# Attention through packed queries, then a squared-ReLU MLP: the order of the first loads, the zero matmuls and the planner's priorities are changed

## The chip, the cores and the metric

The kernel runs on one core of one Trainium2 chip. The metric is the device time of one execution in microseconds (us), as the median of several runs, beside a profiled execution whose span and trace are read here. The engines are PE (TensorE, the matmuls), PEld (its weight loads), DVE (VectorE), ACT (ScalarE), POOL (GpSimd) and SP (SyncE, which here only issues transfers). "L434" is line 434 of the kernel.

## What is computed

```python
def _attn_ref(q, k, v, p):              # q, k, v: (8, 8, 576, 64); p: (8, 8, 32, 64)
    scale = 1.0 / np.sqrt(q.shape[-1])
    def sm_attn(qq, kk, vv):
        s = scale * np.matmul(qq, kk.transpose(0, 1, 3, 2))
        s = s - np.max(s, axis=-1, keepdims=True)
        a = np.exp(s)
        a = a / (np.sum(a, axis=-1, keepdims=True) + 1e-09)
        return np.matmul(a, vv)
    p_packed = sm_attn(p, k, v)          # 32 packed queries look at 576 keys
    return sm_attn(q, p_packed, p_packed)  # 576 queries look at the 32 packed rows

def _moe_ref(x, w_in, w_out):            # x: the attention output as (4608, 512)
    r = np.maximum(x @ w_in, 0.0)        # w_in: (512, 2048)
    return (r * r) @ w_out               # w_out: (2048, 512)
```

The inputs are float32, the matmuls run in bfloat16, the output is float32 of shape (4608, 512).

## The kernel before

**Work of one batch.** There are 8 batches of 8 heads; heads go in two groups of four (qd 0 and 1). For batch b the steps are:

- Lk, Lq, Lv: loads of keys, queries and values. Tk and Tq: their transposes on DVE (L425, L422).
- S1.b.qd: scores of the packed queries, PE L434 and L436; then maximum on DVE (L440), exponential on ACT (L444), division on DVE (L450, L451).
- E.b.qd: transposes of these weights on PE (L457) and a copy out of PSUM. PV.b.qd: times the values (PE L472). XT.b: copy out, spread over the array (PE L484), four blocks into `pq_bd`.
- M.b.c: the packed rows are multiplied into w_in, one 512-wide quarter c of d_ff at a time (PE L501), and cast to bfloat16. So the second attention and the first MLP matmul become one product with M.
- S2.b: scores of the 576 queries against the 32 packed rows (PE L533, L522, L540), maximum (L552), difference (L557), exponential (L563), sum (L569), reciprocal (L570), product (L575); N.b: transposes of the result (PE L584, L586) and a copy.
- F1: the hidden layer (PE L599; for batch 0 L612 in two parts of tokens, named FA.0.j and F1.0.j, j = 0 to 7), ReLU and square.
- F2.t: output tile t of 128 tokens, sixteen matmuls 128x512 over d_ff (PE L655, the last tile in halves at L672), copied out and stored by SP.

**Who sets the order.** All engine orders are fixed when the program is built. A small planner (`Plan`) simulates the steps with written-down durations and emits each instruction at the moment it chooses. `plan.stream` gives it lists of steps; only the head of each list is a candidate. Of the ready candidates it takes the one with the smallest priority: `level(st)`, a number by kind of step and batch, plus the step's entry in the table `TABLE["o"]`. `late` is the priority of a step's later pieces, `lean` a bias for or against ACT where a piece may run on ACT or DVE. `plan.base` says when each engine and the transfers may first be used. Where the planned gap before a PE piece exceeds 0.3, `fills` puts zero matmuls into it (`keep_clock`, L322, 128x256 on a tile of zeros), the gap divided by 0.2135 when the planned start lies before `plan.warm`, and by 0.109 after it. This stops at the first F2 step.

**Loads.** The packed queries of batches 0 and 1 (`p_f`, float32) are loaded by one transfer issued on ACT's queue (L896), then cast (P.0, L901), transposed (L364) and spread by ACT into the block-diagonal `pT_bd` (X.0, L370). The keys of batch 0 go by two transfers on SP's queue (L390) into a part of `gT` used as a stage, and are cast to bfloat16 by DVE or ACT (L338 or L336). All other loads are issued by POOL, with casting, at most 8 in flight (the "dq" slots). They form one stream in the order of `ORDER`: v0 q0 i0 a0 a1 a2 a3 b0 b1 k1 b2 b3 v1 i1 b4 b5 q1 b6 b7 p2, then keys, values and queries of batches 2 to 7. Here a0 to a3 are the quarters of w_in (two transfers each, L402), b0 to b7 the eighths of w_out (L406), i0 and i1 two groups of POOL's own set-up work (the identity and `perm`; zeros for later batches).

PSUM has 8 banks: `HB` are the pairs (0,1) and (2,3), for S1 and F1; `AB` are 4 and 5, for E, PV, S2's rest and N; `OB` are 6 and 7, for F2. The zero matmuls write to bank 7.

Of the kernel before, what the change touches and what calls it, by code (L numbers as in the profile page):

```python
# [14 lines left out]
P = 128  # L15
# [11 lines left out]
TURN = 0.098  # L27


class Piece:  # L30
    __slots__ = ("step", "stage", "k", "alts", "start", "end", "alt", "prio")
# [20 lines left out]
class Plan:  # L52
# [13 lines left out]
    def forward(self):  # L66
# [37 lines left out]
        while heap:  # L104
# [4 lines left out]
            while True:  # L109
# [18 lines left out]
                for pr, i, pc, x in cand:  # L128
                    best = None
                    for a, (e, us, _) in enumerate(pc.alts):  # L130
                        b = t if e == "-" else max(t, busy.get(e, 0.0))
                        v = b + us + (pc.step.lean if e == "ACT" else 0.0)
                        if best is None or v < best[0]:
                            best = (v, b, a, e, us)
# [3 lines left out]
                    if e != "-" and any(p < pr - self.margin and r < t + self.wait and r - t < 0.5 * us and any(z[0] == e for z in q.alts) for p, r, q in soon):  # L138
                        continue
# [59 lines left out]
    def aim(self):  # L199
        for steps in self.streams:  # L200
            for st in steps:
                st.prio = self.prio.get(st.key, self.level(st))
                st.late = st.prio - (50.0 if st.key[:2] == "F2" else 0.25)
                if st.key[0] == "L":
                    st.late = -200.0 + 1e-3 * steps.index(st)
                st.lean = self.lean.get(st.key, 0.0)

    def level(self, st):
        c, b = (st.key.split(".") + ["0"])[:2]
        c = c if c in self.levels else c[0]  # L210
        return self.levels[c] + (10.0 * int(b) if c != "F2" else 10.0 * int(b) / 4.5)
# [27 lines left out]
TABLE = {'o': {'P.0': 278.96, 'X.0': 259.57, 'P.2': 1061.15, 'X.1': 1343.17, 'I': 212.19, 'I2': 150.43, 'Tk.0.0':  # L239
    439.21, 'Tk.0.1': 861.87, 'Tk.1': 967.23, 'Tk.2': 849.12, 'Tk.3': 482.64, 'Tk.4': -762.08, 'Tk.5': 249.26,  # L240
    'Tk.6': 200.49, 'Tk.7': 414.65, 'Tq.0.0': 127.48, 'Tq.0.1': 1090.31, 'Tq.1': 1115.72, 'Tq.2': 121.32, 'Tq.3':
    -623.59, 'Tq.4': 1404.69, 'Tq.5': 150.43, 'Tq.6': 318.39, 'Tq.7': 722.94, 'S1.0.0': 318.19, 'S1.0.1': -1312.39,
    'E.0.0': 965.39, 'E.0.1': 477.51, 'PV.0.0': 623.26, 'PV.0.1': 854.68, 'XT.0': 12.62, 'S1.1': 457.12, 'E.1':
    333.58, 'PV.1': 201.8, 'XT.1': 362.5, 'S1.2': -1278.15, 'E.2': -839.66, 'PV.2': 678.99, 'XT.2': 387.66, 'S1.3':
    770.89, 'E.3': 361.87, 'PV.3': 1076.32, 'XT.3': 1087.1, 'S1.4': 131.97, 'E.4': 436.3, 'PV.4': 241.92, 'XT.4':
    221.39, 'S1.5': 445.52, 'E.5': 270.8, 'PV.5': 1091.84, 'XT.5': 1117.46, 'S1.6': -38.5, 'E.6': 843.53, 'PV.6':
    864.69, 'XT.6': 134.96, 'S1.7': -443.87, 'E.7': 458.02, 'PV.7': 616.8, 'XT.7': 472.98, 'M.0.0': 1090.96,
    'M.0.1': 1052.64, 'M.0.2': 1085.1, 'M.0.3': 1364.91, 'M.1': 151.72, 'M.2': -1054.29, 'M.3': 573.24, 'M.4':
    41.37, 'M.5': 789.8, 'M.6': 841.24, 'M.7': 864.69, 'S2.0.0': 467.42, 'SB.0.1': 1184.08, 'N.0.0': 198.08,
    'SC.0.2': 938.26, 'N.0.1': 367.35, 'S2.1': 79.58, 'C.1': -1246.42, 'N.1': -521.83, 'S2.2': 456.6, 'C.2':  # L250
    -1097.77, 'N.2': -1321.15, 'S2.3': 399.95, 'C.3': 138.17, 'N.3': 152.94, 'S2.4': 449.75, 'C.4': 134.0, 'N.4':
    1028.99, 'S2.5': 1029.01, 'C.5': 870.47, 'N.5': -920.75, 'S2.6': 486.06, 'C.6': 143.24, 'N.6': -1112.63, 'S2.7':
    279.5, 'C.7': -1418.52, 'N.7': 729.26, 'FA.0': 718.18, 'F1.0': 464.76, 'F1.1': 137.13, 'F1.2': 457.22, 'F1.3':
    715.7, 'F1.4': 433.32, 'F1.5': -719.33, 'F1.6': -585.4, 'F1.7': 134.0, 'F2.0': 1114.48, 'F2.2': 474.61, 'F2.4':
# [19 lines left out]
def kernel_impl(tc, q, k, v, p, w_in, w_out, out):  # L274
    nc = tc.nc
# [708 lines left out]
```

## Time and profile before

| | us |
|---|---|
| three runs | 258.64, 259.18, 259.11; median 259.11 |
| the profiled execution, its own time | 260.67 |
| its span in the trace | 258.9 |
| PE busy | 247.9 (96%), 2154 instructions |
| DVE, ACT, POOL busy | 173.9 (67%), 163.4 (63%), 46.5 (18%) |
| zero matmuls (L322) among PE | 16.3, 97 instructions |
| transfers | 29.06 MB; about 200 GB/s in the first 95 us, under 90 GB/s after |

The page divides the span into 40 slices of 6.5 us. PE shows 7 tenths in the first, 9 or more in the others until the last, which shows 4. The granted clock column stands at full throughout. A group line of the page gives line, engine, operation, written tile and read tiles, shapes and count, then the busy time, the mean time of one in ns, and the idle time of the engine just before them with what ended it. A timeline line gives start, length, engine, line, operation and count, with idle time before it in brackets. A stretch line of the table by windows gives for each engine the busy time in that stretch and the count.

### The profile page before, as it was taken

The numbers are of one execution on the slowest core, as the hardware profiler recorded it, in microseconds if no ns is written. First come the engines' busy times: TensorE is split into PE (matmuls) and PEld (weight loads), VectorE is DVE, ScalarE is ACT, GpSimd is POOL, SyncE is SP. The second block draws the span as 40 slices with busy tenths as digits, with TensorE's granted clock in tenths as the row PEclk, the third lists the DMA queues.
The fourth block names the chain that finished last, engine by engine and source line by source line (L and its number), as shares of the span: only waits on it lengthen the run. The fifth ranks groups of instructions, "written<-read, shape, count | busy, mean of one in ns | idle before, by whom it ended". The sixth has DMA issues, their size and how long they took to land.

```text
span 258.9 us, 5498 instructions
## 1 busy us (share of the span) xinstructions
PE 247.9 (96%) x2154; PEld 146.9 (57%) x2185; DVE 173.9 (67%) x341; ACT 163.4 (63%) x281; POOL 46.5 (18%) x79
## 2 busy tenths in 40 slices
PE   7799999999999999999999999999999999999994
PEld 4477565465644766465665656456563665366452
DVE  3659679998579599956884686927879367546210
ACT  2346988746974758787874844589437784768101
POOL 8646954332424300000000000000000000000000
PEclk9999999999999999999999999999999999999999
DMA  7999999999999994411103111130030211121123
GB/s 219 197 202 207 202 208 197 215 248 227 207 212 231 230 219 96 88 43 44 41 8 86 32 41 43 43 81 22 24 83 7 75 43 28 34 62 41 42 73 90
DMA packets 26617, 29.06 MB, mean 112 GB/s; under 512 B 5472, under 2 KB 18016, under 8 KB 26592
## 3 DMA queue, kind: packets, MB, share of 16 engines
q0 software_dynamic: 18672, 17.96, 42.4%
q1 hardware_dynamic: 7296, 10.56, 14.5%
q8 instruction: 17, 0.28, 0.4%
q10 hardware_dynamic: 624, 0.20, 0.3%
q14 instruction: 8, 0.07, 0.1%
HBM read 37.22 MB, written 9.44 MB: 180 GB/s over the span
## 4 chain that ended last, share of the span: by engine, by line
PE 85%; DVE 6%; ACT 4%; DMA 2%; issue 1%; DVEq 0%; ACTq 0%
PE pb L655 43%; PE ps L599 21%; PE ps L434 3%; PE ps L522 2%; PE ps L612 2%; PE pb L322 2%; PE ps L501 2%; PE pb L472 2%; DMA p_f<-in_p_dram 2%; PE pb L457 2%; PE pb L672 1%; PE pb L501 1%; PE pb L584 1%; ACT gT L628 1%; ACT r L621 1%
## 5 line engine op out<-in xcount | busy, mean ns | idle before, releaser
L655 PE MATMUL pb<-w_out_b,gT 128*128 128x512 bf16 x529 | 137.7, 379 | 1.8 <-issue 0.8
L637 ACT ACTIVATE r<-ps 128x576 bf16<-128x576 f32 x112 | 70.9, 652 | 23.8 <-PE ps L599 20.8
L655 PEld LDWEIGHTS <-gT 128*128 128x128 bf16 x560 | 52.1, 98 | 49.9 <-issue 4.1
L647 DVE TENSOR_TENSOR gT<-r 128x576 bf16<-128x576 bf16 x112 | 49.7, 455 | 33.4 <-ACT r L637 32.5
L599 PE MATMUL ps<-a,M 128*128 128x288 bf16 x448 | 70.7, 286 | 0.5 <-ACT r L637 0.2
L599 PEld LDWEIGHTS <-M 128*128 128x128 bf16 x448 | 43.1, 98 | 22.1 <-issue 2.2
L336 ACT COPY o_sb<-pb 128x512 f32<-128x512 f32 (+1 forms) x19 | 11.0, 577 | 19.7 <-PE pb L655 17.0
L336 ACT CAST M<-ps 128x1024 bf16<-128x1024 f32 (+1 forms) x20 | 17.4, 883 | 8.1 <-PE ps L501 8.1
L338 DVE COPY o_sb<-pb 128x512 f32<-128x512 f32 (+1 forms) x18 | 12.0, 666 | 15.1 <-PE pb L655 8.5
L444 ACT ACTIVATE e1x<-ps,n 128x576 bf16<-128x576 f32 x16 | 11.8, 742 | 15.0 <-DVE n L440 15.0
L322 PE MATMUL pb<-zero 128*128 128x256 bf16 x97 | 16.3, 328 | 1.1 <-DVE zero L341 1.1
L563 ACT ACTIVATE e<-d 128x1152 bf16<-128x1152 f32 (+2 forms) x10 | 9.7, 973 | 11.8 <-DVE d L557 11.6
L440 DVE TENSOR_REDUCE n<-ps 128x1 f32<-128x576 f32 x16 | 11.7, 752 | 5.9 <-PE ps L436 5.8
L336 ACT CAST M<-pb 128x512 bf16<-128x512 f32 x27 | 14.7, 598 | 0.0
L399 POOL DMA_DIRECT2D v_b<-in_v_dram x16 | 11.3, 704 | 14.4 <-DMA k_b<-in_k_dram 9.6
L383 POOL DMA_DIRECT2D q_b<-in_q_dram x16 | 8.9, 562 | 26.5 <-DVE kT L425 16.5
L434 PE MATMUL ps<-kT,pT_bd 128*128 128x512 bf16 x32 | 10.5, 417 | 2.9 <-ACT pT_bd L370 2.2
L322 PEld LDWEIGHTS <-zero 128*128 128x128 bf16 x97 | 10.7, 116 | 4.4 <-DVE zero L341 1.1
L569 DVE TENSOR_REDUCE t<-e 128x36 f32<-128x1152 bf16 (+2 forms) x10 | 11.0, 1099 | 3.2 <-ACT e L563 3.1
L425 DVE STREAM_TRANSPOSE kT<-k_b 128x576 f32<-128x576 f32 x16 | 11.7, 757 | 0.0
L422 DVE STREAM_TRANSPOSE qT<-q_b 128x576 f32<-128x576 f32 x16 | 11.7, 756 | 0.0
L575 DVE TENSOR_TENSOR n<-e,r 128x1152 bf16<-128x1152 bf16 (+2 forms) x10 | 11.1, 1110 | 0.2
(72 smaller groups left out, 236.7 us busy)
## 6 DMA issues: line engine op xcount, KB each, us to landing
out_dram<-o_sb SPq DMA_DIRECT2D x140, 64.0 KB, 1.7
q_b<-in_q_dram POOLq DMA_DIRECT2D x16, 288.0 KB, 11.6
k_b<-in_k_dram POOLq DMA_DIRECT2D x14, 288.0 KB, 12.2
v_b<-in_v_dram POOLq DMA_DIRECT2D x8, 320.0 KB, 11.6
v_b<-in_v_dram POOLq DMA_DIRECT2D x8, 256.0 KB, 11.6
w_in_b<-in_moe_w_in_dram POOLq DMA_DIRECT2D x8, 256.0 KB, 10.5
w_out_b<-in_moe_w_out_dram POOLq DMA_DIRECT2D x8, 256.0 KB, 10.0
gT<-in_k_dram SPq DMA_DIRECT2D x2, 576.0 KB, 5.5
```

What stands on the lines that cost most here:

```text
L322: nc.tensor.matmul(half(7)[:, :2 * P], lhsT=zero[:, :P], rhs=zero, start=True, stop=True)
L336: nc.scalar.copy(dst, src)
L338: eng.tensor_copy(dst, src)
L422: nc.vector.transpose(self.qT[:, qd].rearrange("p s x -> p (s x)").bitcast(F32), self.t.q[qd][:].bitcast(F32))
L425: nc.vector.transpose(kT[:, qd].rearrange("p s x -> p (s x)").bitcast(F32).rearrange("p (x a j2) -> p j2 x a", a=32, j2=2), self.t.k[qd][: ...
L434: nc.tensor.matmul(main, lhsT=w[dh], rhs=kT[:, qd, :GM * P, dh], start=(dh == 0), stop=(dh == 1))
L440: nc.vector.tensor_reduce(self.n1[:, qd:qd + 1], self.ps1[qd], axis=AX.X, op=ALU.max, negate=True)
L444: nc.scalar.activation(e1x[:, qd], self.ps1[qd], ACT.Exp, bias=self.n1[:, qd:qd + 1], accum_out=self.d1[:, qd:qd + 1])
L599: nc.tensor.matmul(ps[:, c], lhsT=a.M[:, qd, fb * FB:(fb + 1) * FB], rhs=a.a2[:, qd, c * HALF:(c + 1) * HALF], start=(qd == 0), stop=(qd = ...
L637: nc.scalar.activation(dst, src, ACT.Relu)
L647: eng.tensor_tensor(out=Att.cols(gT[:, fb, o:o + S]), in0=r, in1=r, op=ALU.mult)
L655: nc.tensor.matmul(po[t], lhsT=gT[:, fb, n0:n0 + P], rhs=w_out_b[:, fb, :], start=(fb == 0), stop=(fb == NFB - 1))
```

## The change

The load of `p_f` moves from ACT's queue to SP's, ahead of the two key loads, and the step LP.0 that stands for it in the planner moves to SP too. The planner's first times for transfers are later, and `warm` goes from 6.6 to 8.0. Steps of batch 0 other than loads and F steps get 1000 subtracted from their priority, and lose their entries in the table. An engine is held idle when a piece with priority below -500 will be ready within 0.2 and would go ahead. The first 21 entries of `ORDER` become streams of their own, with priorities of their own in the table, so that their order is free; by level plus table entry it is now v0, q0, b0, a0, i0, a1, k1, a2, b1, a3, b2, v1, q1, b3, b4, p2, b5, b6, b7, k2, i1. The F1 steps of batch 0 split into two streams, F2 tiles 2 and 3 get streams of their own and one more bank each (5 and 3) for their choice, and `lean` is kept per stage. The rest of the table is a new set of numbers. No matmul, activation or vector operation on data is added or taken away.

```diff
+RUSH, RWAIT = -500.0, 0.2
...
-                        v = b + us + (pc.step.lean if e == "ACT" else 0.0)
+                        v = b + us + (pc.lean if e == "ACT" else 0.0)
...
-                    if e != "-" and any(p < pr - self.margin and r < t + self.wait and r - t < 0.5 * us and any(z[0] == e for z in q.alts) for p, r, q in soon):
+                    if e != "-" and any((p < pr - self.margin and r < t + self.wait and r - t < 0.5 * us or p < RUSH and p < pr - 0.2 and r < t + RWAIT)
+                                        and any(z[0] == e for z in q.alts) for p, r, q in soon):
...
                 if st.key[0] == "L":
-                    st.late = -200.0 + 1e-3 * steps.index(st)
-                st.lean = self.lean.get(st.key, 0.0)
+                    st.late = -200.0
+                for stage in st.pieces:
+                    for pc in stage:
+                        pc.lean = self.lean.get(f"{st.key}/{pc.stage}", 0.0)
 
     def level(self, st):
+        if st.key in self.levels:
+            return self.levels[st.key]
         c, b = (st.key.split(".") + ["0"])[:2]
         c = c if c in self.levels else c[0]
+        if b == "0" and c[0] not in "FL":
+            return self.levels[c] - 1000.0
...
+TABLE = {'o': {'P.2': -67.67, 'X.1': -587.68, 'Lv0': -1157.14, 'Lq0': -1041.87, 'Li0': -521.7, 'La0': -551.11,
+    'La1': -484.86, 'La2': -478.43, 'La3': -360.63, 'Lb0': -1014.54, 'Lb1': -383.71, 'Lk1': -502.47, 'Lb2': -361.33,
+    'Lb3': -254.42, 'Lv1': -351.57, 'Li1': 62.92, 'Lb4': -268.21, 'Lb5': -245.36, 'Lq1': -296.26, 'Lb6': -237.1,
...
-                        banks=OB if fb == 0 else ()) for fb in range(last)]
+                        banks=(OB + {2: [(5,)], 3: [(3,)]}.get(t, [])) if fb == 0 else ()) for fb in range(last)]
...
+        EARLY = 21
...
-        plan.base.update(DVE=2.4, POOL=1.2, ACT=2.1, SP=0.3, DMA=3.2, DMB=1.9, PE=1.1)
-        nc.scalar.dma_start(p_f, p_of(0, 2))
+        plan.base.update(DVE=2.4, POOL=1.2, ACT=2.1, SP=0.7, DMA=4.4, DMB=2.35, PE=1.1)
+        nc.sync.dma_start(p_f, p_of(0, 2))
...
-        plan.stream([Step("LP.0", [[[("ACTQ", 0.5, lambda: None)]]], lag=2.4)])
...
+            for st in g:
+                st.key = "L" + x
+            plan.levels["L" + x] = -200.0 + 5.0 * i
+            if i < EARLY:
+                plan.stream(g)
+            else:
+                ld += g
+        plan.stream([Step("LP.0", [[[("SP", 0.45, lambda: None)]]], lag=1.8)] + load_k32())
...
-        plan.stream(sum([f1_steps(b) for b in range(B)], []))
-        plan.stream(sum([f2_steps(t) for t in range(0, NT, 2)], []))
-        plan.stream(sum([f2_steps(t) for t in range(1, NT - 1, 2)] + [fz_steps(NT - 1, h) for h in range(2)], []))
+        plan.stream(fh_steps(0))
+        plan.stream(fh_steps(1) + sum([f1_steps(b) for b in range(1, B)], []))
+        plan.stream(f2_steps(2))
+        plan.stream(f2_steps(3))
+        plan.stream(sum([f2_steps(t) for t in range(0, NT, 2) if t != 2], []))
+        plan.stream(sum([f2_steps(t) for t in range(1, NT - 1, 2) if t != 3] + [fz_steps(NT - 1, h) for h in range(2)], []))
         plan.use(TABLE)
-        plan.warm, plan.keep = 6.6, keep_clock
+        plan.warm, plan.keep = 8.0, keep_clock
```

## The prediction

> **What bounds the kernel now.** I read the busy shares first, then a table of stretches, then the chain of waits and the timeline of the first 14 us. From the page:
>
> ```profile
> PE 247.9 (96%) x2154; PEld 146.9 (57%) x2185; DVE 173.9 (67%) x341; ACT 163.4 (63%) x281; POOL 46.5 (18%) x79
> L322 PE MATMUL pb<-zero 128*128 128x256 bf16 x97 | 16.3, 328 | 1.1 <-DVE zero L341 1.1
> ```
>
> The table of stretches, for all instructions and then for the zero matmuls alone (first the stretch and its length, then PE busy):
>
> ```profile
> 0.00:28.00 28.00, 24.01 (x233) 16.47 (x234) 17.29 (x40) 12.91 (x27) 19.09 (x34) 1.00 1.11 206
> 28.00:240.00 212.00, 208.69 (x1840) 122.17 (x1868) 154.02 (x298) 148.44 (x252) 27.36 (x46) 1.00 0.54 104
> 240.00:255.40 15.40, 15.17 (x86) 8.24 (x85) 2.60 (x5) 1.86 (x4) 0.00 (x0) 1.00 0.25 65
> ...
> 8.85:11.81 2.96, 2.96 (x14) 1.94 (x14) 1.00 1.12 209
> 13.82:15.30 1.48, 1.48 (x15) 1.17 (x12) 1.00 1.23 203
> 0.00:28.00 28.00, 16.31 (x97) 10.65 (x97) 1.00 1.11 206
> ```
>
> From 28 to 255.4 us PE is busy 208.69 + 15.17 = 223.86 of 227.4: 98.4%, with 3.5 us free. Before 28 us all 97 zeros lie, so real work there is 24.01 - 16.31 = 7.7 of 28 us: 20.3 us are lost. After the last matmul come 3.5 us of copy and store (255.4 to 258.9). So the kernel is a PE-bound stretch behind a head in which PE waits for one batch's chain. What shortens the head, or puts real work into it, comes off the end nearly one for one; what lengthens it is added.
>
> The head's chain of waits begins so (start, length, what):
>
> ```profile
> 0.78 4.68 DMA p_f<-in_p_dram
> ...
> 7.43 0.42 ACT pT_bd L370
> 7.85 0.04 issue
> 7.90 1.03 PE ps L434 x2
> 8.93 0.11 PE ps L436 x2
> 9.04 2.99 PE pb L322 x14
> 12.02 0.85 PE ps L434 x2
> ```
>
> Two faults are seen. The first scores (7.90) wait for the packed queries, which land at 5.46. The second scores wait behind 14 zeros. Their keys were ready before: the timeline has the second transpose of the keys, L425, from 9.75 for 0.77, so to 10.52, and the second scores at 11.82, 1.3 us later. The zeros were laid out at 0.109 each and took 2.96 / 14 = 0.21; those at 13.82 took 1.48 / 15 = 0.10. PE is at half its speed until about 13.6, which the clock column (1.00) doesn't show.
>
> After that the chain is latency alone: second maximum 13.02, PV to 17.03, S2 at 18.96, N.0.0's matmuls 24.01, first FA at 25.17. Whatever moves the second scores moves S2.
>
> **The change, part by part.**
>
> *Packed queries first on SP.* Issuing `p_f` takes 0.45 us and comes ahead of the keys. Of the transfers of the keys the trace says:
>
> ```profile
> DMA to landing us min/median/max: 4.3/5.5/6.7
> ```
>
> The first was issued at 0.75 and landed at 5.1, the second at 1.21 and landed at 7.9. `p_f` shared that time with them; alone in front it can't land later than 5.46, and after P.0, L364 and X.0 (7.90 - 5.46 = 2.4 us) would even then allow scores at 7.9; I take 3.5 + 2.4 = 5.9, so keys become the limit. The keys land between 5.1 (the bytes of both loads are the same as before) and 5.1 + 0.45 (issue) + 0.78 (the 0.3% of 16 engines' 258.9 us that ACT's queue used) = 6.3. I take 5.5, the issue time alone. Two casts (0.82) and a transpose (0.78) plus 0.1 of hops make 7.2. Gain on the first scores 0.7 us, bounds 8.0 (loss 0.1) and 6.8 (gain 1.1).
>
> *Fewer zeros between first and second scores.* The second keys land at 7.9 to 8.4. Casts took 1.08, transpose 0.77, and the first maximum (0.76) may lie ahead of it on DVE: second scores at 7.9 + 1.08 + 0.77 + 0.1 = 9.85 at best, 10.3 + 0.76 = 11.1 at worst; I take 10.2. The gap now divides by 0.2135, not 0.109, so the same gap gives 7 zeros, not 14, or 1.5 us, which ends by 8.3 + 1.5 = 9.8: PE is no longer late. Gain on the second scores 11.8 - 10.2 = 1.6 us (0.7 to 2.0).
>
> *Zeros after the second scores.* PE was at half speed until 13.6. The wait from the second scores' end to the next transposes is now open (first maximum, exponential, division: 0.76 + 0.74 + 0.19 + 0.6 = 2.3), and a planned gap of about 1.5 us is filled with 13 zeros meant for 0.109; at 0.213 these last 2.8, 1.4 too long. I take a third of it, 0.5 (0 to 1.4). So S2 comes 1.6 - 0.5 = 1.1 earlier. Values and queries don't hold it: the four transfers ahead of w_in have landed by 13 us, when POOL goes on (L402 at 12.99) on the landing of the second `q_b`, and the two transposes of 0.77 follow.
>
> *Precedence of the first batch.* In S2's chain DVE did the second half's difference (21.65, 0.69) ahead of the first half's sum, which was ready at 21.7: 0.6 us. ACT cast M (21.96 to 23.03) ahead of the second exponential, ready at 22.34: 0.6 us. I take 0.4 of the sum on the path, bounds 0 and 1.2.
>
> *Load order.* b0 and k1 go ahead of most of w_in. POOL's wait lines give a landing every 1.3 us, 2.8 us for a pair of keys. With b0, a0 and a1 ahead of it k1 lands 1.3 + 5.2 + 2.8 = 9.3 us after the queries (12.7), at 22; now its second half is issued at 18.63 and lands some 10 us later, at 29. So batch 1's scores and transposes (2 x 0.61 + 2 x 0.22 + 2 x 0.44 = 2.5 us, at 31.9 to 37.9 in the trace) can replace some of the 34 zeros that follow 20 us (3.7 us). I take 1.0 us, bounds 0 and 2.5. Against it, a2 lands 1.3 + 2.8 = 4.1 us later and a3 5.4: its last, issued at 12.99, landed at 23.6 and would land at 29.0. M.0.3 ran at 27.20 and its cast needed 1.29, so FA.0.6 can't start before 29.0 + 0.4 + 1.3 = 30.7, where it started at about 30.4 before. That was free then; with the chain 1.5 us earlier it bites. Batch 1 covers part: I charge 0.5 (0 to 2.0, where nothing covers it).
>
> *Streams, banks, the new table.* The same instructions in another order. They can only win in the 3.5 us free after 28 us, and can lose as much: 0, bounds -1.0 and +1.0.
>
> Sum: 1.1 + 0.4 + 1.0 - 0.5 = 2.0 us off. The profiled execution took 260.67 (span 258.9 and 1.8 around it): 258.7. The median of the runs shown lies 1.56 below it, so 257.1 for the median.
>
> **A rule that speaks against it.** The zeros' row is 0.213 until 13.6 and 0.10 after. The Trainium skill, "TensorE: Matmul & The Clock Gate", Part 1, says that PE's clock is halved until it was busy through a window of about 3.4 us, and that the windows run freely. The trace agrees: gaps at 5.7 to 7.9 kept it slow, and it turned fast 5.7 us after 7.9. By the rule fewer zeros may leave it slow longer; by the rows alone I charge 0.5. This is rival C.
>
> **The rivals.** *B, no change.* The head is bound by transfers as well: about 206 GB/s throughout, and w_out's last eighth lands after everything in front of it whatever the order. If the late w_in costs its full 2.0 us and batch 1 covers nothing: 1.1 + 0.4 - 2.0 = -0.5, and a free table's half: 259.1 + 0.5 - 0.5 = 259.1. For it: the full transfers until 97 us. Against: PE had real work of 98% from 28 us on while w_out was still landing.
>
> *C, slower: the clock.* With only 7 zeros behind the first scores, PE idles between them and the second scores and stays at half speed through to S2. The place is 10 to 18 us. There 30 zeros stood (13.3 to 18.3); each is 0.104 longer: 3.1 us, and E's two sets of transposes 0.27 each and S2 0.5 make 4.1. Against the 1.6 + 0.4 gained earlier, with 0.9 of the zeros' excess lying in planned slack, it is 4.1 - 2.0 - 0.9 = 1.2 lost: 260.3. It decides once more than about 20 zeros in that place run at 0.21 (20 x 0.104 = 2.1, the gain). For it: the same fault happened with 14. Against: an overshoot is itself busy time, and before, the clock rose while the zeros ran.
>
> *D, the queries land no earlier.* If `p_f` on SP still lands at 5.4, the first scores stay at 7.9 and the zeros' gain is left, with no new work in the head: 1.3 - 0.5 = 0.8: 258.3. Against: it is at the head of its queue.
>
> **How the numbers follow.** A, the forecast, 0.53; B 0.17; C 0.22; D 0.08. No change means within 0.2%, 0.52 us, about what a measurement of this kernel can tell (its three runs span 0.54). A and D are faster, save 0.01 of D; a sixth of B lies over 0.52 faster, a third over 0.52 slower, and C is slower. So faster 0.53 + 0.07 + 0.03 = 0.63, same 0.09, slower 0.28. A's own range goes from 254.8 (the precedence in full, 0.8 more; the overlap at 2.0, 1.0 more; no charge for w_in, 0.5 more) to 258.5 (the zeros' excess in full, 0.9 less; w_in at 1.0, 0.5 less). For 8 in 10 it is stretched up to 260.2, which takes in B, D and half of C; 0.11 of C and 0.06 of A below are left out.
>
> **What would show it.** Right: P.0's cast on DVE starts before 4.5 us, not 5.48; first scores near 7.2; at most 8 zeros between first and second scores, second scores by 10.5; S2 by 18; the first FA by 24; fewer than 75 zeros in all; PE's real work before 28 us 2 us more than 7.7; from there 98% as before. Wrong: keys landing after 6.3; zeros at 0.21 beyond 15 us (C); PE free or idle at FA.0.6 to wait for M.0.3 (B); more than 5 us free after 28 us, which would lay it on the new table. If the head is 2 us shorter and the end isn't, the bound I read is wrong.

## The result, and the profile after

The changed kernel takes 261.92 us (261.32 to 266.92, four runs) and the kernel before 259.14 us (258.64 to 259.24, four runs). The ratio is 1.0098, with a 95% interval of [1.0072, 1.0123]: it is 0.98% slower, where 257.1 us was forecast. The profile taken at 266.92 was disturbed and is left out of the ratio, so what follows reads a second profiled execution of each kernel: 262.44 us with a span of 260.6 for the changed one, 259.18 us with 257.4 for the one before.

First the busy shares of the changed kernel and the group of its zero matmuls:

```profile
PE 249.9 (96%) x2180; PEld 144.3 (55%) x2180; DVE 175.2 (67%) x340; ACT 164.2 (63%) x282; POOL 46.9 (18%) x79
L332 PE MATMUL pb<-zero 128*128 128x256 bf16 x92 | 15.9, 332 | 1.1 <-DVE zero L351 1.1
```

There are 92 zeros instead of 97, so the change took five away, not a quarter of them. The table of stretches of the changed kernel (after the stretch: length, busy time of PE, PEld, DVE, ACT, POOL, granted clock, share of the transfer engines, GB/s):

```profile
0.00:28.00 28.00, 22.05 (x206) 15.26 (x207) 19.34 (x40) 11.66 (x23) 21.23 (x38) 0.88 1.10 204
28.00:43.00 15.00, 14.49 (x152) 8.70 (x149) 10.56 (x22) 13.62 (x27) 7.49 (x11) 1.00 1.35 201
43.00:100.00 57.00, 56.42 (x514) 32.01 (x515) 47.19 (x93) 40.86 (x68) 18.19 (x30) 1.00 1.19 216
```

The same for its zero matmuls alone (PE, PEld, DVE):

```profile
0.00:28.00 28.00, 15.85 (x92) 10.15 (x92) 0.17 (x1) 0.88 1.10 204
10.94:15.10 4.16, 3.17 (x14) 1.95 (x14) 0.00 (x0) 0.50 1.18 203
```

Both tables for the kernel before, all instructions and then the zeros:

```profile
0.00:28.00 28.00, 24.05 (x243) 16.98 (x244) 18.74 (x43) 14.30 (x30) 19.34 (x34) 0.94 1.11 207
28.00:43.00 15.00, 14.46 (x152) 8.67 (x150) 11.33 (x24) 13.62 (x25) 9.84 (x17) 1.00 1.34 202
43.00:100.00 57.00, 56.94 (x510) 32.45 (x506) 46.35 (x86) 38.68 (x68) 17.05 (x29) 1.00 1.20 222
```

```profile
0.00:28.00 28.00, 15.37 (x97) 10.25 (x97) 0.17 (x1) 0.94 1.11 207
```

Real work of PE before 28 us is 22.05 - 15.85 = 6.20 us, against 24.05 - 15.37 = 8.68: 2.5 us less, where 2 us more was forecast. From 28 to 43 us both leave 0.5 us free; from 43 to 100 us the changed kernel leaves 0.58 and the other 0.06. These 2.5 + 0.5 are most of the 3.2 us between the spans, though the 0.5 is loose: the profile that the prediction read, of the kernel before, leaves 0.70 free from 43 to 100 us. The clock column shows part of the reason: 0.88 against 0.94 in the first stretch, and 0.50 while the 14 zeros run.

Where does the head lose it? PE of the changed kernel from the second scores on (start, length, engine, line, tiles, and in brackets the idle time before it and what ended it):

```profile
10.93 1.01 PE L444 MATMUL ps<-kT,pT_bd 128*128 128x512 bf16 x2 [0.96 <-DVE kT L435]
11.74 0.31 PE L446 MATMUL ps<-kT,pT_bd 128*128 128x64 bf16 x2
11.86 3.17 PE L332 MATMUL pb<-zero 128*128 128x256 bf16 x14
15.49 0.45 PE L467 MATMUL pb<-ident,e1n 128*128 128x128 bf16 x5 [0.46 <-DVE r L460]
```

The kernel before, the same place:

```profile
7.88 2.76 PE L322 MATMUL pb<-zero 128*128 128x256 bf16 x14
10.42 1.06 PE L434 MATMUL ps<-kT,pT_bd 128*128 128x512 bf16 x2
11.28 0.31 PE L436 MATMUL ps<-kT,pT_bd 128*128 128x64 bf16 x2
11.40 0.60 PE L457 MATMUL pb<-ident,e1n 128*128 128x128 bf16 x5
```

The second scores are 0.5 us later (10.93 against 10.42), but the transposes E.0.0 behind them are 4.1 us later (15.49 against 11.40). E.0.1, which S2 needs too, is 2.2 us later (16.11 against 13.91). Both wait for e1n, the result of a division on DVE. (The last bracket names r, the reciprocal of the next group, which ends beside it; e1n itself is written until 15.43.) DVE of the changed kernel:

```profile
12.09 0.76 DVE L450 TENSOR_REDUCE n<-ps 128x1 f32<-128x576 f32 x1 [0.57 <-PE ps L446]
...
12.95 2.48 DVE L461 TENSOR_SCALAR e1n<-e1x,r 128x576 bf16<-128x576 bf16 x1
...
15.53 0.37 DVE L461 TENSOR_SCALAR e1n<-e1x,r 128x576 bf16<-128x576 bf16 x1
```

The kernel before:

```profile
9.93 0.56 DVE L451 TENSOR_SCALAR e1n<-e1x,r 128x576 bf16<-128x576 bf16 x1
```

The same instruction takes 2.48 us at 12.95 and 0.37 at 15.53. POOL of the changed kernel at that time:

```profile
10.73 2.68 POOL L358 MEMSET pT_bd<- 128x3072 bf16 x1
13.32 1.94 POOL L360 MEMSET v_b<- 64x512 bf16 x4
```

POOL clears the tiles of later batches (group i1, step I2) from 10.73 to 15.26 us. The first division is issued into that and ends at 15.43, and the second follows it. In the kernel before the same memsets run from 24.54 to 29.09 us:

```profile
24.54 2.68 POOL L348 MEMSET pT_bd<- 128x3072 bf16 x1
```

They were moved by the new load streams, because i1 is now one of them. By priority it stands last, and yet it runs ahead of the keys of batch 1: unlike a load it needs no load slot, so it can be the only ready step on POOL while the loads wait. The code reads so; it wasn't tried apart. (The first division also starts later, 12.95 against 9.93, because the first maximum now stands behind the transpose of the second keys on DVE, and these land later. That alone doesn't set S2, since the second division ended last in the kernel before, at 13.86.)

Last, the transfers of the keys of batch 0, changed kernel and then the kernel before:

```profile
DMA to landing us min/median/max: 5.2/6.4/7.6
```

```profile
DMA to landing us min/median/max: 3.7/4.5/5.4
```

They land at 6.45 and 9.37 us against 4.46 and 6.58.

The two executions against each other, with the first start of each step in us:

| | first scores | second scores | E.0.0 | S2 | first FA | end of span |
|---|---|---|---|---|---|---|
| before, the profile of the prediction | 7.90 | 11.82 | 12.79 | 18.96 | 25.17 | 258.9 |
| before, second profile | 7.35 | 10.42 | 11.40 | 17.57 | 23.77 | 257.4 |
| changed, second profile | 8.31 | 10.93 | 15.49 | 19.89 | 25.63 | 260.6 |

The span grows by 3.2: 2.3 up to S2, 0.5 off between S2 and the first FA (6.20 against 5.74), and 1.3 more from there to the end (233.6 against 235.0). The first row also shows that the profile behind the prediction was about 1.4 us long in the head.

### The profile page after: what moved, and what is told of

The parts are those of the page before. It is cut to its first block, busy times and chain, and to the rows that moved or that the text cites. A ratio compares the mean times of both kernels' runs of the same rounds, so it can differ in the third digit from the quotient of the medians.

```text
span 265.1 us, 5521 instructions
## 1 busy us (share of the span) xinstructions
PE 249.3 (94%) x2180; PEld 144.6 (55%) x2180; DVE 177.5 (67%) x340; ACT 164.4 (62%) x282; POOL 46.7 (18%) x79
## 4 chain that ended last, share of the span: by engine, by line
PE 86%; DVE 6%; ACT 3%; DMA 3%; issue 0%; SPq 0%; DVEq 0%
PE pb L665 46%; PE ps L609 21%; DMA gT<-in_k_dram 3%; PE ps L532 2%; PE ps L444 2%; PE pb L482 2%; PE pb L467 2%; PE ps L511 2%; DVE k_b L348 2%; PE pb L332 2%; PE ps L622 1%; PE pb L682 1%; PE pb L594 1%; PE pb L511 1%; ACT r L631 1%; ACT gT L638 1%
## 5 line engine op out<-in xcount | busy, mean ns | idle before, releaser
L665 PE MATMUL pb<-w_out_b,gT 128*128 128x512 bf16 x560 | 145.2, 380 | 0.0
L647 ACT ACTIVATE r<-ps 128x576 bf16<-128x576 f32 x112 | 71.0, 653 | 17.1 <-PE ps L609 13.6
L657 DVE TENSOR_TENSOR gT<-r 128x576 bf16<-128x576 bf16 x112 | 50.6, 457 | 38.4 <-ACT r L647 37.1
L346 ACT CAST M<-ps 128x1024 bf16<-128x1024 f32 (+1 forms) x19 | 16.8, 897 | 5.5 <-PE ps L511 5.5
L454 ACT ACTIVATE e1x<-ps,n 128x576 bf16<-128x576 f32 x16 | 11.9, 742 | 12.9 <-DVE n L450 12.9
L348 DVE COPY o_sb<-pb 128x512 f32<-128x512 f32 (+1 forms) x17 | 11.2, 657 | 12.0 <-DMA out_dram<-o_sb 6.1
L332 PE MATMUL pb<-zero 128*128 128x256 bf16 x92 | 15.2, 322 | 1.1 <-DVE zero L351 1.1
L346 ACT CAST M<-pb 128x512 bf16<-128x512 f32 x29 | 15.7, 597 | 0.0
L332 PEld LDWEIGHTS <-zero 128*128 128x128 bf16 x92 | 9.9, 115 | 3.6 <-DVE zero L351 1.1
L631 ACT ACTIVATE r<-ps 128x512 bf16<-128x512 f32 (+1 forms) x14 | 8.7, 649 | 4.9 <-PE ps L622 4.9
```

The costliest lines, as they stand in the source:

```text
L332: nc.tensor.matmul(half(7)[:, :2 * P], lhsT=zero[:, :P], rhs=zero, start=True, stop=True)
L346: nc.scalar.copy(dst, src)
L348: eng.tensor_copy(dst, src)
L454: nc.scalar.activation(e1x[:, qd], self.ps1[qd], ACT.Exp, bias=self.n1[:, qd:qd + 1], accum_out=self.d1[:, qd:qd + 1])
L647: nc.scalar.activation(dst, src, ACT.Relu)
L657: eng.tensor_tensor(out=Att.cols(gT[:, fb, o:o + S]), in0=r, in1=r, op=ALU.mult)
```

## Experiments

Each ratio is to the kernel before, run on the same chip, with its 95% interval. Repeats of both kernels gave the second profiles above.

> The kernel before once more, for a second trace. The profiled execution used for the prediction took 260.67 us, 1.5 more than the median. Theory: the difference lies in the head (later landing of the keys, the 14 zeros at half clock), so this trace, if it takes 259.0 to 259.4, has its second scores 1 to 2 us earlier than 11.82. Rival: the head is the same to 0.3 us and the difference lies elsewhere.

> The changed kernel once more, for a trace of an execution near its median (261.9 us). Theory: DVE's cast of the second keys is held by POOL's memsets here too, by 1 to 4 us according to when the keys land (8 to 10 us), and second scores start at 11 to 14. Rival: the cast takes 0.45 us and the time is lost elsewhere.

Measured: the first theory held, with second scores at 10.42, 1.4 us earlier than in the profile of the prediction. The second missed as it stands. In this execution the memsets start behind the casts, and the cast takes its usual time:

```profile
9.39 0.46 DVE L348 CAST k_b<-gT 128x576 bf16<-128x576 f32 x1 [1.13 <-DMA gT<-in_k_dram]
```

The memsets hold the division instead.

### The memsets, moved back

e1: the changed kernel, with the code of I2 emitted behind the second half of batch 1's values.

```diff
+            if p.step.name == "I2":
+                held = fn
+                continue
             fn()
+            if (p.step.name, p.stage) == ("Lv.1.1", 0):
+                held()
```

> The changed kernel, with POOL's five memsets of step I2 (zeros for later batches, 4.6 us) issued behind the loads of batch 1's values instead of at 9.6 us. Theory (DVE's cast of the second keys, 5.08 us at 9.38, was held by these memsets): the cast takes about 0.45 us, the second scores start near 11 us instead of 15.4, the head is some 4.4 us shorter and the time is 256 to 258 us, under before. Rival 1 (the length of the cast comes from the late landing of the keys, 9.36, and not from POOL): the cast stays near 5 us and the time near 261. Rival 2 (the half clock is the cause): second scores early, but the zeros still run at 0.21 past 20 us and the time is 259 to 261.

Measured: 260.85 us, 1.0052 [1.0030, 1.0074]. About half of the loss is gone, where the theory expected all of it and more (256 to 258). The time lies in rival 2's range, but not for its reason in this trace, whose half clock ends at 11.13 us. The division takes 0.37 us again, in DVE's timeline of e1:

```profile
11.59 0.37 DVE L466 TENSOR_SCALAR e1n<-e1x,r 128x576 bf16<-128x576 bf16 x1
```

S2 starts at 16.72 (changed kernel 19.89, before 17.57), the first FA at 22.45. The last quarter of w_in lands at 29.21 us, and at 29.34 in the changed kernel, so the memsets don't cost by holding back these loads of POOL.

e19: the same kernel once more, as a control for e16 below.

> The changed kernel with the memsets behind the values of batch 1 and all 14 zeros, as in e1, on the same chip as e18: the control for e16. Theory (14 zeros at half speed cost time): 1.0052 as in e1, 260.5 or more, with 7 of 12 executions below a mean clock of 0.99. Rival (e1's share of executions with two windows at half clock was chance, and e16's 1.0008 is what the moved memsets alone give): 1.001 to 1.003, 259.4 to 260.0, with 2 or 3 of 12 below 0.99.

Measured: 260.43 us, 1.0033 [1.0008, 1.0058], between theory and rival; one of 12 executions had a mean clock below 0.99, where e1 had 7. This is the same kernel on two chips, so e1's share says little of the kernel. The moved memsets are worth 0.46% to 0.65%. (One stretch of 3.41 us at half clock takes 0.0066 off the mean over 258 us: about 0.993 is one such stretch on record, 0.987 two, 0.980 three. A mean of 1.000 doesn't show that there was none: the profile of the prediction has 1.000, and zeros of 0.21 us until 13.6.)

### The memsets, put into the kernel before

e3: the kernel before, I2 emitted behind the first two loads of w_in, so that POOL clears from 7.4 to 11.9 us.

```diff
+        early = next(p for p in out if p.step.name == "I2")
...
-            fn()
+            if p is not early:
+                fn()
+            if (p.step.name, p.stage) == ("LWI.0.1", 0):
+                early.alts[early.alt][2]()
```

> The kernel before, with step I2's memsets issued right behind the first two w_in loads, near 7.3 to 12 us, over the casts of its second keys (7.93 to 9.01). Theory: a DVE cast there is held until 12, the second scores start near 13.5 instead of 11.82 and the time is 260.5 to 263. Rival (POOL's memsets don't hold DVE): all as before, 259.1, or a little more for w_in loads issued 4.6 us later.

Measured: 264.32 us, 1.0207 [1.0189, 1.0226], and nothing else of the change is in this kernel. DVE:

```profile
7.07 5.77 DVE L342 CAST k_b<-gT 128x576 bf16<-128x576 f32 x2
```

and POOL:

```profile
7.38 2.68 POOL L352 MEMSET pT_bd<- 128x3072 bf16 x1
9.97 1.95 POOL L354 MEMSET v_b<- 64x512 bf16 x4
```

Two casts that take 0.97 us in the repeat of the kernel before take 5.77. The first of them runs from 7.07 to 12.24, 0.3 us past the last memset: DVE waits through all five memsets, not through one. S2 starts at 22.54 us, 5.0 later, and the span is 5.0 longer. Of these 5.0 the second scores have 3.8 (14.24 against 10.42); the rest comes behind them, where 16 zeros at half clock take 3.37 us instead of 1.91, after PE had idled 4.73 us. The last quarter of w_in lands 1.05 us later (24.64), and PE doesn't wait for it. So memsets over a DVE cast are enough to cost time, and the loss was more than the 260.5 to 263 expected.

### Which operations of DVE are held

e2: the changed kernel, both casts of the second keys on ACT.

```diff
-  ("DVE", 0.36, lambda qd=qd, i=i: L[0].cast_k(qd, i, V)),
+  ("DVE", 0.36, lambda qd=qd, i=i: L[0].cast_k(qd, i, A if qd else V)),
```

> The changed kernel, with both halves of the second keys cast by ACT; POOL's memsets stay at 9.6 us. Theory (memsets of POOL hold DVE's cast): ACT does the two casts in 2 x 0.67 us, to 10.7; DVE's transpose of the keys then takes its usual 0.78 if POOL holds only casts and copies, so second scores near 11.6 and a time of 257 to 258.5; if POOL's memsets hold every DVE instruction from SBUF to SBUF, the transpose ends at 14.5 and the time stays near 261. Rival 1 (late landing): 261 either way.

Measured: 261.93 us, 1.0109 [1.0089, 1.0129]: no gain. The 257 to 258.5 expected if only casts and copies are held is missed. DVE (POOL's memsets run from 11.32 to 15.86):

```profile
11.32 0.78 DVE L435 STREAM_TRANSPOSE kT<-k_b 128x576 f32<-128x576 f32 x1 [3.90 <-ACT k_b L346]
...
13.31 0.76 DVE L450 TENSOR_REDUCE n<-ps 128x1 f32<-128x576 f32 x1 [0.57 <-PE ps L446]
...
14.18 1.85 DVE L461 TENSOR_SCALAR e1n<-e1x,r 128x576 bf16<-128x576 bf16 x1
```

The transpose (0.78) and the maximum out of PSUM (0.76) run at their usual length beside a memset; the division doesn't. Taking the casts away from DVE saves nothing here: the next operation that can be held stands behind them (and the second keys landed 0.65 us later in this execution than in the repeat).

### The packed queries on SP

e7: the kernel before with this part alone.

```diff
-        nc.scalar.dma_start(p_f, p_of(0, 2))
+        nc.sync.dma_start(p_f, p_of(0, 2))
```

> The kernel before with one edit: the packed queries are issued by SP ahead of the keys, all orders else as before. As predicted (first scores 0.7 us earlier, second scores bound by the second keys and the 14 zeros): 258.0 to 259.2. Theory now: SP's order lets POOL's first transfers start about 1.2 us earlier (4.3 instead of 5.5) and these delay the second keys to 8 to 10 us, so second scores come at 10.5 to 12.5 and the time is 259.0 to 260.5.

Measured: 259.74 us, 1.0020 [1.0007, 1.0033]: a little slower, as the theory had it, and not the prediction (its profile is of the longest of 12 executions, 260.82). The transfers of the keys, and that of the packed queries:

```profile
DMA to landing us min/median/max: 4.8/5.8/6.9
```

```profile
DMA to landing us min/median/max: 2.3/2.3/2.3
```

The packed queries land at 3.07 instead of 4.9 us, and the keys at 6.05 and 8.65 instead of 4.46 and 6.58. First scores at 7.90, against 7.35. This holds over the traces of this study: in the eight with `p_f` on SP the first keys land at 5.3 to 6.5 and the second at 7.8 to 10.0 us; in eleven of the twelve with it on ACT at 4.2 to 4.6 and 6.3 to 7.4 (the twelfth is the profile that the prediction read, with 5.1 and 7.9). POOL's first packets, which share the transfer engines, start at 4.0 to 4.7 us in the first kind and at 5.4 to 5.6 in the second.

e4: e1 with `p_f` back on ACT's queue.

```diff
-        nc.sync.dma_start(p_f, p_of(0, 2))
+        nc.scalar.dma_start(p_f, p_of(0, 2))
```

> As the first kernel (memsets late), and the packed queries' load back on ACT's queue. If the packed queries on SP bring what the prediction said (first scores 0.7 to 1 us earlier, second keys not earlier), this is 0 to 1 us slower than the first kernel, because the second scores wait for the second keys either way; if SP's order delays the second keys (9.36 instead of 7.91), this is up to 1.4 us faster than the first kernel.

Measured: 260.50 us, 1.0043 [1.0031, 1.0055], inside the range of e1 and e19. In the changed kernel this part is worth nothing that can be told apart: second scores at 9.96, against 9.57 and 9.43 there.

### The zero matmuls

e8: the kernel before with `warm` at 8.0, so 7 zeros instead of 14 between first and second scores.

```diff
-        plan.warm, plan.keep = 6.6, keep_clock
+        plan.warm, plan.keep = 8.0, keep_clock
```

> The kernel before with one edit: warm at 8.0 instead of 6.6, so 7 zeros instead of 14 between first and second scores. As predicted: PE no longer late for the second scores, 0.5 to 1.3 us faster, 257.8 to 258.7. Rival (the clock): with fewer zeros the clock rises a window later and the time is the same or up to 1.5 us longer.

Measured: 259.12 us, 0.9992 [0.9978, 1.0005]. No difference, where the prediction expected 0.5 to 1.3 us; second scores at 10.22.

e6: e4 with `warm` at 12, which leaves 7 zeros instead of 14 behind the second scores.

```diff
-        plan.warm, plan.keep = 8.0, keep_clock
+        plan.warm, plan.keep = 12.0, keep_clock
```

> The changed kernel with POOL's memsets late, the packed queries on ACT's queue, and warm at 12.0 instead of 8.0, so that the 14 zeros behind the second scores become 7. In the trace without this the 14 took 3.09 us (10.93 to 14.02) at half clock while the weights were ready for E.0.0 at 12.4. Theory: E.0.0 starts 1 us earlier in such runs and the time is 259.3 to 260.2. Rival: the clock rises later for it and nothing is won, 260.5.

Measured: 259.86 us, 1.0024 [1.0013, 1.0036].

e16: e1 with the same line at 12.

> The changed kernel with the set-up zeros of I2 behind the values of batch 1 (as in e1) and the bound of half-speed planning at 12 instead of 8: 7 zero matmuls instead of 14 behind the second scores, more elsewhere none. Theory (part of what e1 still loses is TensorE at half clock through a second window, because it idles in the head): the recorded mean clock is below 0.99 in at least 7 of 12 executions as in e1, since there are fewer zeros, not more, and the time is 260.5 to 261. Rival (14 half-speed zeros only delay the transposes): 260.2 to 260.5, 0.2% under e1, whatever the clock.

Measured: 259.50 us, 1.0008 [0.9993, 1.0023]. My theory was wrong and the rival right in its direction: with the memsets out of the way, 7 zeros fewer behind the second scores take off another 0.25% (against e19) to 0.44% (against e1), and from e4 to e6 it is 0.19%. The intervals of e19 and e16, and of e4 and e6, overlap, so the size is loose; the direction is the same in all three comparisons, two of which share e16. With both mended the changed kernel can't be told from the one before.

e18: the changed kernel with that line alone, memsets where they are.

> The changed kernel with its memsets where they are and the bound of half-speed planning at 12 instead of 8, so that 7 zero matmuls instead of 14 stand behind the second scores. Theory (the zeros are a cost of their own, 0.3 to 0.45%, beside the memsets' 0.46%): ratio to the kernel before about 1.0055 to 1.007, 260.6 to 261.0. Rival (the zeros cost nothing while the memsets hold the division that the transposes wait for, since that ends last anyway): 1.009 to 1.010, 261.5 to 261.9.

Measured: 262.56 us, 1.0122 [1.0081, 1.0163]. Both ranges missed, but the rival's reading is the nearer: the same edit now gains nothing. PE of e18:

```profile
10.32 1.68 PE L332 MATMUL pb<-zero 128*128 128x256 bf16 x7
14.21 0.71 PE L467 MATMUL pb<-ident,e1n 128*128 128x128 bf16 x5 [2.20 <-DVE r L460]
```

and the stretch between, in the columns used above:

```profile
10.90:15.10 4.20, 2.00 (x14) 1.28 (x12) 4.13 (x6) 0.98 (x3) 4.20 (x8) 0.50 1.17 195
```

While the memsets hold the division, fewer zeros mean 2.20 us of idle PE, and the clock records of this execution stand at half from 9.03 to 19.27 us, three windows of 3.41. All six executions have a mean clock of 0.973 to 0.984; the repeat of the changed kernel, with 14 zeros, was at half from 8.70 to 15.53.

### A shorter head with the old orders

e14: the kernel before, with every later order kept. DVE does the transpose of the second keys (Tk.0.1; both keys are batch 0's) ahead of the first maximum, ACT casts the second half of the second keys, and 3 zeros instead of 14 stand between first and second scores. e15 is the same with all 14 zeros.

```diff
+        mx, tk = at["S1.0.0", 1], at["Tk.0.1", 0]
...
+            if p is mx or p is tk:
+                o = tk if p is mx else mx
+                fn = o.alts[o.alt][2]
...
-                self.keep(self.fills(p.start - free.get(e, 0.0), p.start))
+                self.keep(3 if p.step.name == "S1.0.1" else self.fills(p.start - free.get(e, 0.0), p.start))
...
-  ("DVE", 0.36, lambda qd=qd, i=i: L[0].cast_k(qd, i, V)),
+  ("DVE", 0.36, lambda qd=qd, i=i: L[0].cast_k(qd, i, A if qd and i else V)),
```

> The kernel before, every order kept but two in the head: DVE takes the second transpose of the first keys ahead of the first maximum and ACT casts the second keys' second half, and 3 zero matmuls instead of 14 stand between the first and the second scores. Theory (the later order gives back what the head gains): with the later order of before, the gain stays. Second scores at about 8.8 us (10.4 in the repeat of the kernel before), S2 at about 16 (17.6), the first FA at about 22.2 (23.8), time 257.5 to 258.5. Rival (the transfers or the later engines set the end): the first FA comes earlier and the time stays at 259.1.

> The same, with all 14 zero matmuls kept between the first and the second scores. If the zeros there cost time by themselves: second scores stay at about 10.4 us, because 14 zeros of 0.2 us end there, and the time stays at 259.1 (at most 0.5 below). If the zeros are free because keys and casts are late anyway: second scores at about 8.8 to 9.5 and the same time as with 3 zeros.

Measured: e14 260.03 us, 1.0028 [1.0009, 1.0046]; e15 259.11 us, 0.9989 [0.9976, 1.0003]. e14 is above both of its ranges; e15 is as expected if the zeros set the second scores (10.34). In e14:

```profile
7.79 0.49 PE L327 MATMUL pb<-zero 128*128 128x256 bf16 x3
8.77 0.61 PE L439 MATMUL ps<-kT,pT_bd 128*128 128x512 bf16 x2 [0.49 <-DVE kT L430]
9.22 0.22 PE L441 MATMUL ps<-kT,pT_bd 128*128 128x64 bf16 x2
10.88 0.45 PE L462 MATMUL pb<-ident,e1n 128*128 128x128 bf16 x5 [1.44 <-DVE e1n L456]
```

The second scores come 1.65 us earlier, E.0.0 only 0.5 and E.0.1 0.9 (13.01): PE now waits for the division. Of the 0.9 us at the first FA (22.87) 0.4 reaches the end of this execution (span 257.0). But 7 of 12 executions had a mean clock of 0.984 to 0.986 and took 259.7 to 260.7; none of the kernel before went below 0.991 on that chip. The profiled one, at 258.79, isn't among the seven. Three more took 259.65 to 261.14 with 1.000 on record, so the clock on record doesn't explain every one.

e17: e14 with 5 zeros between the scores, and 6 more in the idle time behind them.

```diff
-                self.keep(3 if p.step.name == "S1.0.1" else self.fills(p.start - free.get(e, 0.0), p.start))
+                self.keep({"S1.0.1": 5, "E.0.0": 6}[p.step.name] if p.stage == 0 and p.step.name in ("S1.0.1", "E.0.0") and p is at[p.step.name, 0] else self.fills(p.start - free.get(e, 0.0), p.start))
```

> e14 with TensorE kept busy in the head: 5 zero matmuls instead of 3 between the first and the second scores and 6 more in the 1.44 us that it idled between the second scores and the first transposes. Theory (e14 has second scores 1.6 us earlier and loses it to a second window at half clock, bred by the idle TensorE): mean clock at 0.991 or more in nearly all executions, first FA at about 22.9, time 258.6 to 259.0. Rival (the window comes from where the free-running windows fall, not from idleness here): clock below 0.99 in half of the executions again, 260.0.

Measured: 258.96 us, 0.9990 [0.9980, 1.0001]; the clock is at 0.992 or more in all 12 executions. The theory held: with the gaps filled no second stretch at half clock is on record, and the loss is gone, so idle PE in the head bred it. PE of e17:

```profile
8.16 1.25 PE L327 MATMUL pb<-zero 128*128 128x256 bf16 x5
9.21 1.06 PE L439 MATMUL ps<-kT,pT_bd 128*128 128x512 bf16 x2
10.07 0.31 PE L441 MATMUL ps<-kT,pT_bd 128*128 128x64 bf16 x2
10.19 0.94 PE L327 MATMUL pb<-zero 128*128 128x256 bf16 x6
10.96 0.44 PE L462 MATMUL pb<-ident,e1n 128*128 128x128 bf16 x5
```

It is the best kernel of the study by its median, and can't be told from the one before.

t_half: the kernel before, the second half of the second keys only on ACT for the planner too, `warm` at 8, all re-planned.

```diff
-  [[("DVE", 0.36, lambda qd=qd, i=i: L[0].cast_k(qd, i, V)),
+  [([("DVE", 0.36, lambda qd=qd, i=i: L[0].cast_k(qd, i, V))] if not (qd and i) else []) +
```

> An attempt to beat both: the kernel before with warm at 8.0 and the second half of the second keys cast by ACT alone, so that DVE transposes these keys ahead of the first maximum. The keys land at 6.6; second scores near 9.0 instead of 10.4; if the rest of the chain follows, 258.0 to 258.7; if the zeros, the queries' transposes or the new layout of later steps take it back, 259.0 to 259.8.

Measured: 259.86 us, 1.0026 [1.0013, 1.0038], with the first FA at 23.03, 0.7 us earlier than in the kernel before. The planner laid the rest out anew, so this alone didn't say where the 0.7 us went.

### The load order

e13: the kernel before, with POOL's loads issued in the order of the changed kernel, and nothing else.

```diff
+        put = {a.step.name: by[b].alts[by[b].alt][2] for a, b in zip(pool, want)}
...
+            if e == "POOL" and p.stage == 0:
+                fn = put.get(p.step.name, fn)
```

> The kernel before with POOL's loads alone in the order of the changed kernel (b0 ahead of w_in, batch 1's keys ahead of its third and fourth quarter, b1 between these); all other engines as before. Theory (late w_in is a cost of its own, rival B of the prediction): the last quarter lands near 28.5 us instead of 23, M.0.2 and M.0.3, which stand in PE's order ahead of the FA steps, wait for it, and with nothing of batch 1 brought forward the time is 260.5 to 262. Rival (w_in was early by enough): 259.0 to 259.6.

Measured: 261.51 us, 1.0096 [1.0078, 1.0114]. The first FA slips from 23.77 to 25.45, while S2 doesn't (17.55). From the list of PE's waits (idle time, count, the longest):

```profile
PE ps L508 <- DMA w_in_b<-in_moe_w_in_dram: 1.3, 2, 0.9
...
PE pb L508 <- DMA w_in_b<-in_moe_w_in_dram: 0.8, 1, 0.8
```

The quarters of w_in arrive late: 2.1 us, what the prediction bounded at 2.0. In the changed kernel, whose orders were made for it, PE waits nowhere for w_in after 20 us.

e5: e4 with the loads planned by `ORDER` again (the table's entries for loads left out).

```diff
-        self.prio = {k: level[k] + d for k, d in z.get("o", {}).items() if k in level}
+        self.prio = {k: level[k] + d for k, d in z.get("o", {}).items() if k in level and k[0] != "L"}
```

> The changed kernel with POOL's memsets late, the packed queries on ACT's queue and the loads in ORDER as before (the table's entries for loads dropped; the planner lays the other engines out anew). If the load order is what is left of the loss (1.0043 without it): 258.7 to 259.8. If it is not: 260.5, or more, since the table's numbers were found for the other load order.

Measured: 261.40 us, 1.0088 [1.0071, 1.0106], slower than e4. Its first FA is at 22.47, earlier than e4's 23.99, and from there to the end it takes 237.1 us, 2.2 more. This doesn't separate the load order, since the table's other numbers were made for the other order.

## Why the prediction was wrong

**The step that failed** is the last term, "Streams, banks, the new table. The same instructions in another order ... 0". Among these instructions are the memsets of group i1, which the change takes from 24.5 us to 10.7. They have no data to do with the head, so only order was seen in the move. They hold DVE's divisions, and these are on the chain that sets S2. Moving them back gives 0.46% to 0.65% (e1, e19), and putting them over a cast of the kernel before costs 2.07% (e3). The same term put the new orders behind the head at 0 and at worst +1.0; from the first FA to the end they take 1.3 us more (see load order below).

**Zeros after the second scores** were priced at 0.5 us with bounds 0 and 1.4. Mechanism and size are near: 14 zeros were planned for 0.109 each and took 3.17 us. Undoing half of them takes off 0.25% to 0.44%, 0.65 to 1.1 us, with the memsets moved (e16 against e19 and e1). With the memsets in place they cost nothing, since the division ends later anyway, and taking them out leaves PE idle (e18). The two causes don't add, but both mended bring the kernel to 1.0008.

**Fewer zeros between the scores**, gain 1.6: fell. "PE is no longer late" held, with 0.96 us idle ahead of the second scores. The gain was sized on an execution in which keys and scores were late: 11.82, where the repeat has 10.42. The 1.56 us that the prediction took off at the end, from its profile to the median, is mostly this late head (11.82 - 10.42 = 1.4), so that 1.4 was counted twice. In e8 the same edit is worth nothing; a larger one, 3 zeros instead of 14, costs 0.39% between e15 and e14.

**Packed queries on SP**, gain 0.7: fell. Their landing was right (3.1 us, forecast 3.5). The keys' was not: they land 1.6 to 2.1 us later with this edit (e7), where 0.45 was charged. The first scores come no earlier.

**Precedence**, gain 0.4: held up to the first FA, but most of it is paid back behind it. From S2 to the first FA the changed kernel takes 5.74 us, in e16 too, the one before 6.20. The third quarter of M stands ahead of the first FA in the kernel before and behind it in the changed one (second profiles, in this order):

```profile
23.18 0.41 PE L501 MATMUL ps<-w_in_b,ppT 64*32 64x512 bf16 x8
```

```profile
30.27 0.41 PE L511 MATMUL pb<-w_in_b,ppT 64*32 64x512 bf16 x8
```

Ahead of the first FA these 0.41 us take the place of zeros; behind it they are added.

**Load order**, +1.0 and -0.5: the landings were right (k1 at 23.09, forecast 22; the last quarter of w_in at 29.34, forecast 29.0), but the balance was not. From the first FA to the end the kernel before takes 233.6 us. The changed kernel takes 235.0, e1 and e19 235.0, e16 235.5: 1.3 to 1.9 us longer, which eats the precedence and what e1 and e16 gain in the head. Late w_in is not what these 1.3 us pay: PE waits nowhere for it, and the stretch is 234.9 to 235.0 whether the first FA is at 22.45 (e1), 23.25 (e19), 25.63 (the changed kernel) or 26.48 (e2), while the last quarter lands at 29.2 to 31.6. Nor does the stretch follow how late the head is: with the old orders it is 233.6 with the first FA at 23.77 and at 28.75 (e3). So the 1.3 us belong to the new orders behind the first FA. The moved matmuls of M are 0.41 of it; what makes up the rest stays open, and e5 doesn't tell.

**The rivals.** C came true in part. In the second profile PE is at half speed from 8.70 to 15.53, two windows, and in the first of them it idles only at C's place: the 0.96 us ahead of the second scores. But the window ends with E.0.0 and not at S2, and E.0.0 waits for the held division at any clock. e18 has three windows, nearly to S2 (19.27, S2 at 19.64); there PE idles behind the second scores as well. What C alone costs wasn't measured. B's late w_in is shown in e13 for the old orders, and not in the changed kernel. D is refuted: the queries do land earlier.

**The bound that was read**, that PE's head comes off the end nearly one for one, held in one direction only, one trace each. A later S2 went to the end in full (e3: S2 5.0 us later, span 5.0 us longer). An earlier one, with the old orders, gave 0.4 of 0.8 to 0.9 (e14, e17).

## What to carry to other kernels

When a reorder moves work of an idle engine, look for what runs beside its new place: on this chip a memset on POOL is not free while DVE casts or scales. Size a gain in the head on more than one profiled execution, since one that is 1.5 us off puts the whole error into the head. Zero matmuls in a gap were worth keeping here as long as the gap was there (e14, e17, e18), and cost only where the work behind them was ready (e16).

## What the runs showed of the hardware

POOL's memsets stop DVE's casts from SBUF to SBUF and its bfloat16 product with a scalar per partition (5.77 us for two casts that take 0.97, 2.48 and 1.85 us for a product that takes 0.37), and not its transposes or its reductions out of PSUM (0.78 and 0.76 beside a memset, e2). The Trainium skill, "SBUF — State Buffer", section "SBUF: two separate sides", says that DVE in a two-port mode and GpSimd take one pair of ports by an exclusive lock, and that the one that comes second is blocked fully. The traces agree on the block; that it lasts over five memsets in a row is more than the page's "for the whole instruction". Which comes first isn't told by these rows: the held cast of e3 is on record from 7.07, 0.3 us ahead of the first memset.

The clock stood at half for stretches of 3.41, 6.83 and 10.24 us. The Trainium skill, "TensorE: Matmul & The Clock Gate", Part 1, has free-running windows of 3413 ns, which agrees. Its advice in the section "Why this matters for your kernels" is to avoid idle gaps above about 3 us. The traces are stricter. In every trace but the one at 266.92 us, with all the idle time of PE inside one window of the head added up, a window at half was followed by another at half in the 5 cases with 0.80 to 2.40 us idle, and by one at full in the 12 cases with 0 to 0.72 us; a window at full was followed by one at half in the 12 cases with 1.92 to 2.65 us, and by full in the 2 cases with 1.74 and 1.86 us. So in this head several short gaps in one window were enough, and a smaller sum was enough while PE was still slow. It fits e14, whose gaps of 0.49 and 1.44 us went with two windows at half, by the mean clock, in 7 of 12 executions, and e17, where they are filled and none shows it.

With the packed queries' transfer on SP's queue instead of ACT's, POOL's first packets start 0.7 to 1.6 us earlier, and the keys land later. Why POOL's queue starts earlier wasn't tried.
